# An attention block written out in ticks: each engine's result is taken up one tick later, and the first FFN quarter takes both chunks of a batch through each weight tile

## The chip, the cores and the metric

The kernel runs on one core of one Trainium2 chip. Its engines are TensorE (PE, matrix products), VectorE (DVE), ScalarE (ACT), GpSimd (POOL) and SyncE (SP, which here only issues transfers). Each engine works through its own list of instructions in the order in which the program was written, and waits at the head of that list for semaphores of the others. The metric is the device time of one execution in microseconds (us), lower is better.

## The reference

Three layers follow each other, all in float32. Batch 2, 8 heads, 768 positions, head size 64, so 512 channels.

```python
# attention: a window of +-15 positions, and 24 summary keys (max over 32 keys) with their mean values
scores_l = scale * q @ k.T                      # kept where |i - j| < 16
scores_s = scale * q @ k_sum.T + log(32)
a = softmax(concat(scores_l masked, scores_s))  # with 1e-9 added to the sum
x = a @ concat(v, v_sum)
# mixing over positions of rank 32, then a feed-forward network (FFN) 512 -> 2048 -> 512
u = x + (x.T @ U @ V).T
x = u + relu(u @ w_ch1) @ w_ch2
# second block: each position mixed with the one before it
xk = mu_k * x + (1 - mu_k) * x_prev;  xr = mu_r * x + (1 - mu_r) * x_prev
out = sigmoid(xr @ w_r) * (relu(xk @ w_k) ** 2 @ w_v)
```

## The kernel before

**Stages.** Attention runs per pair of heads: four pairs make a batch, and a pair is cut into three groups of 256 queries, so `attention(b)` has twelve groups. `attention(0)` runs alone. Then the first of four FFN quarters (512 hidden channels, four tiles of 128) is done for batch 0, and `attention(1)` is laid between its matrix products. After that come the same quarter for batch 1, three more quarters for both batches, and the second block. Weights come as 64-bit words and are converted on the way: loaded (L404), split by ACT (L415, L416), worked on by DVE (L421, L424, L425), added by POOL (L431), rounded to a high part by ACT (`whi`, L456) and a low part by POOL (`wlo`, L460). Each product of the FFN is three matmuls (high x high, high x low, low x high).

**One group of attention.** `s_stage` (L179): PE forms the scores of a group in two PSUM banks. `soft_stage` (L201): DVE adds the mask and takes the maximum (L208), ACT the exponential (L212), four times each. `t_stage` (L215): PE transposes, ACT copies to `pt` (L221). `v_stage` (L224): PE multiplies with the window's values `vcat` (L234), and DVE divides by the sum (L238, L239). Once per pair: `k_prep` (L136), in which DVE takes the summary keys `ks` (L140) and POOL lays windows and summary keys out in `kw` (L146 to L148); `sum_v` (L152, `vs`) and `spread_v` (L158), in which DVE sums values, PE turns them, ACT scales them into `vm` (L163) and POOL copies them to `vcat` (L164); and the mixing over positions, `g_stage`, `g2_stage`, `u_stage` (L251 to L287), whose results are `uhi` and `ulo`. In the first pair `turn_v` makes the window values on PE and ACT; other pairs load them (`load_vw`).

**What sets the order.** A plan of ticks, one per group (L301 to L381). In tick i stand the scores and soft stage of group i, the transpose of group i-2, the product with the values of group i-4 and parts of the mixing; then the steps that are not PE's (loads, `k_prep`, `sum_v`) and `d`, which takes so many slots from `side`, the list of weight conversions. A slot moves each of its blocks one step through load, ACT, DVE, POOL, ACT and POOL. The numbers in `at(tick, when, ...)` sort the steps of a tick. After `attention(0)` the FFN's generators give the order: after each half of an FFN tile (`f1`, into the hidden layer, or `f2`, out of it), two steps of `attention(1)` follow, and 1.2 slots of `side`.

**PSUM.** Eight banks, four under each of two names. `gen` holds scores and the products of `f1`, `acc` the accumulators of `f2` and, in `attention(0)`, transposes, values and mixing. In `attention(1)` all attention steps use `gen`. A step that needs a bank waits until the last reader of what stood there is through. For `f1` the last reader is DVE's subtraction to `hl` (L494).

Of the kernel before, what the change touches and what calls it, by code (L numbers as in the profile page):

```python
# [23 lines left out]
R = 32  # L24
# [38 lines left out]
def build(tc, I, out):  # L63
# [34 lines left out]
    vcat = [a_p.tile([128, NT, 2, D + 1], F32, name=f"vcat{i}", bufs=1) for i in range(3)]  # L98

    T_AT, V_AT = 2, 4  # L100
    NPT = V_AT - T_AT + 1
    pts = [a_p.tile([128, 512], F32, name=f"pt{i}", bufs=1) for i in range(NPT)]
# [7 lines left out]
    for i in range(3):  # L110

        nc_p.memset(vcat[i][KW:KC + 1], 0.0)
        nc_p.memset(vcat[i][:, :, :, D:D + 1], 1.0)
# [19 lines left out]
    def load_vw(n):  # L133
        nc.sync.dma_start(out=vcat[n % 3][0:KW], in_=I["vw"][n])
# [23 lines left out]
    def spread_v(n, tag):  # L158

        ps = bank(tag)  # L160
        nc_t.matmul(ps[KW:KC, 0:128], vs_t.pop(n), ident, start=True, stop=True)
        vm = a_p.tile([128, 2, D], F32, name="vm", bufs=2)
        nc_s.activation(vm[KW:KC].rearrange("p h d -> p (h d)"), ps[KW:KC, 0:2 * D], AF.Copy, scale=1.0 / BLK)  # L163
        nc_p.tensor_copy(vcat[n % 3][KW:KC, :, :, 0:D], vm[KW:KC].unsqueeze(1).to_broadcast([NB, NT, 2, D]))  # L164

    def turn_v(n, g, tag):

        ps = bank(tag)
        for j in range(4):
# [3 lines left out]
            vcat[n % 3][0:KW, 4 * g:4 * g + 4, :, 0:D], ps[0:KW].rearrange("p (t h d) -> p t h d", t=4, h=2)  # L173
# [3 lines left out]
    pt_t = {}  # L177

    def s_stage(n, g, tag):  # L179

        ps = [bank(tag) for _ in range(2)]
# [17 lines left out]
        return ps  # L199

    def soft_stage(n, g, ps):  # L201
        P = a_p.tile([128, 4, KC], F32, name="P", bufs=T_AT + 1)
        nm = a_p.tile([128, 4], F32, name="nm", bufs=3)
        for j in range(4):
# [6 lines left out]
            )  # L211
            nc_s.activation(P[:, j], P[:, j], AF.Exp, bias=nm[:, j:j + 1], scale=-1.0)  # L212
        p_t[n, g] = P

    def t_stage(n, g, tag):  # L215
        P = p_t.pop((n, g))
# [3 lines left out]
        pt = pts[(3 * n + g) % NPT]  # L220
        nc_s.copy(pt[0:KC], ps[0:KC])  # L221
        pt_t[n, g] = pt

    def v_stage(n, g, tag):  # L224
        if g == 0:
            x_t[n] = x_p.tile([128, NP, 128], F32, name="xn", tag="xn", bufs=2)
# [3 lines left out]
        for a in range(2):  # L230
            for h in range(2):
                for e in range(2):
                    o = (2 * a + h) * 128 + 64 * e
                    nc_t.matmul(  # L234
                        o4[64 * e:64 * e + 64, a, h], pt[0:KC + 1, o:o + 64], vcat[n % 3][0:KC + 1, 4 * g + 2 * a + e, h], start=True, stop=True,
                    )
        rec = a_p.tile([128, 2, 2, 1], F32, name="rec", bufs=3)
# [22 lines left out]
    def g2_stage(n, tag):  # L260
# [5 lines left out]
        nc_v.tensor_tensor(  # L266
            out=gst[2 * R:3 * R], in0=ps[2 * R:3 * R, 0:128], in1=gst[2 * R:3 * R].bitcast(F32), op=ALU.subtract
# [3 lines left out]
    def u_stage(n, c, tag):  # L271
# [15 lines left out]
        nc_v.tensor_tensor(out=ulo[:, d], in0=ps[:, 0:CH], in1=uhi[:, d].bitcast(F32), op=ALU.subtract)  # L287
# [13 lines left out]
    def attention(b):  # L301

        pairs = range(4 * b, 4 * b + 4)
# [6 lines left out]
        end = len(groups)  # L310
        for i, (n, g) in enumerate(groups):
            at(i, 0, "s", n, g)
            if b or i < end - 4:
                at(i + T_AT, 1, "t", n, g)
                at(i + V_AT, 4, "v", n, g)
                if g == NG - 1:
                    for j, t in enumerate(G_AT):
                        at(i + V_AT + t[0], t[1], "u", n, j)
        if b == 0:

            n = pairs[-1]
            for tick, when, what, *args in (
                (end - 2, 1, "t", n - 1, 2), (end - 1, 1, "t", n, 0), (end, 0.0, "v", n - 1, 2), (end, 1.0, "t", n, 1),
                (end, 1.2, "t", n, 2), (end, 2.0, "v", n, 0), (end, 2.2, "u", n - 1, 0), (end, 2.4, "v", n, 1),
                (end, 2.6, "u", n - 1, 1), (end, 2.8, "v", n, 2), (end, 3.0, "u", n - 1, 2), (end, 3.2, "u", n, 0),
                (end, 3.3, "u", n - 1, 3), (end, 3.4, "u", n, 1), (end, 3.5, "u", n, 2), (end, 3.6, "u", n, 3),
            ):
                at(tick, when, what, *args)
        for n in pairs:
            i = 3 * (n - 4 * b)  # L330
            at(i + 1, 4.5, "sp", n)
            for g in range(NG if n < N_TR else 0):
                at(i + 1 + g, 4.6, "tv", n, g)
        steps = [
# [5 lines left out]
        ]  # L340
        if b:
            steps = []
            for n in range(pairs[1], pairs[-1] + 1):
                steps += [
                    (3 * n - 15, (("k", n), ("lk", n + 1), ("lq", n + 1))), (3 * n - 14, (("sv", n), ("lt", n + 1))),
                    (3 * n - 12, (("lv", n + 1),)),
                ]
        for t, jobs in steps:
            for j, (what, n) in enumerate(jobs):
                if what == "d" or n < 4 * B:  # L350
                    at(t, 6 + 0.1 * j, what, n)
        for tick in sorted(plan):
            steps = sorted(plan[tick], key=lambda x: x[0])
            soft = None
            for k, (_, what, args) in enumerate(steps):
                n = args[0]
                if what in side_steps:
                    side_steps[what](*args)
                    continue
                if what == "s":  # L360
                    soft = (*args, s_stage(*args, tags["s"]))
                    if k + 1 < len(steps) and steps[k + 1][1] == "t":
                        continue
# [469 lines left out]
```

## Time and profile before

| | |
|---|---|
| median of three runs | 557.81 us (556.53 to 558.03) |
| the profiled execution | 555.79 us, span of its instructions 554.0 us |
| PE busy | 519.1 us, 94% of the span |
| DVE, ACT, POOL busy | 316.7, 251.6 and 210.6 us |
| `attention(0)`, until the first FFN matmul | 0 to 60.5 us |
| first FFN quarter of batch 0 with `attention(1)` | 60.5 to 138.6 us |
| all the rest | 138.6 to 554.0 us |

The profiled execution took 1.8 us more than its span; its time is 2.0 us under the median of the three runs. A busy engine is not yet an engine at its peak: PE has two clock levels (1.2 and 2.4 GHz), and at the lower one the same matmul takes about twice as long and still counts as busy. The row of granted clocks tells the level.

### The profile page before, as it was taken

The page shows a single profiled execution, that of the slowest core. Times are in us where ns is not written, and L with a number is a line of the kernel's source. Part 1 is how long each engine was busy: PE and PEld are TensorE (multiplying, and loading weights), DVE is VectorE, ACT ScalarE, POOL GpSimd, SP SyncE. Part 2 cuts the span into 40 slices and gives each one's busy share as a digit, 9 for nine tenths or more (in the row PEclk, how much of TensorE's full clock was granted, in tenths as well). Part 3 has the DMA queues.
Part 4 walks back from the last instruction along what each step waited for, and adds up shares of the span by engine and source line. Part 5 has one row for each costly group of instructions (what it writes and reads, how often), then busy time and mean ns, then how long its engine had stood idle before and what let it go on. Part 6 is the DMA issues. An engine that isn't in the chain of part 4 may idle for free.

```text
span 554.0 us, 8939 instructions
## 1 busy us (share of the span) xinstructions
PE 519.1 (94%) x3468; PEld 475.6 (86%) x3468; DVE 316.7 (57%) x703; ACT 251.6 (45%) x532; POOL 210.6 (38%) x190
## 2 busy tenths in 40 slices
PE   5777488999999999999999999999999999999997
PEld 4555365887999999999999999999888888888885
DVE  5686767544376267755778247746676542542322
ACT  4768366542245144543554144533558543542221
POOL 6354365330077936662666236214352120120000
PEclk9979869999999999999999999999999999999999
DMA  8962393200043023341343123012200100100101
GB/s 270 315 207 77 93 309 108 76 2 1 1 146 127 32 76 117 112 144 48 114 153 112 41 76 115 1 37 78 77 0 1 57 2 0 58 0 1 57 1 57
DMA packets 15129, 45.71 MB, mean 83 GB/s; under 512 B 2656, under 2 KB 2912, under 8 KB 15088
## 3 DMA queue, kind: packets, MB, share of 16 engines
q1 hardware_dynamic: 14912, 44.92, 24.9%
q8 instruction: 27, 0.44, 0.3%
q10 hardware_dynamic: 144, 0.18, 0.2%
q14 instruction: 14, 0.11, 0.1%
q0 software_dynamic: 32, 0.05, 0.0%
HBM read 42.00 MB, written 3.15 MB: 81 GB/s over the span
## 4 chain that ended last, share of the span: by engine, by line
PE 83%; DVE 6%; ACT 5%; DMA 2%; POOL 2%; issue 1%; SPq 0%; POOLq 0%; ACTq 0%; DVEq 0%
PE acc L510 24%; PE gen L489 24%; PE gen L607 12%; PE acc L629 12%; PE gen L591 5%; ACT P L212 2%; DMA kt<-kt 2%; PE gen L196 1%; PE gen L234 1%; PE gen L219 1%; POOL vcat L164 1%; DVE C L424 1%; DVE P L208 1%; PE acc L234 1%; DVE A L425 1%
## 5 line engine op out<-in xcount | busy, mean ns | idle before, releaser
L431 POOL TENSOR_TENSOR A<-C,A 128x512 int32<-128x512 int32 (+1 forms) x54 | 70.9, 1313 | 99.3 <-DVE A L425 97.7
L460 POOL TENSOR_TENSOR wlo<-A,whi 128x512 fp32r<-128x512 f32 x52 | 75.7, 1456 | 49.3 <-ACT whi L456 49.1
L489 PE MATMUL gen<-uhi,whi 128*128 128x384 f32 x256 | 88.3, 345 | 0.0
L510 PE MATMUL acc<-hh,whi 128*128 128x384 f32 x256 | 87.5, 342 | 0.6 <-ACT hh L493 0.6
L489 PE MATMUL gen<-uhi,wlo 128*128 128x384 f32 x256 | 87.0, 340 | 0.0
L489 PE MATMUL gen<-ulo,whi 128*128 128x384 f32 x256 | 86.9, 340 | 0.0
L510 PE MATMUL acc<-hh,wlo 128*128 128x384 f32 x256 | 86.6, 338 | 0.0
L510 PE MATMUL acc<-hl,whi 128*128 128x384 f32 x256 | 86.6, 338 | 0.0
L494 DVE SCALAR_TENSOR_TENSOR hl<-gen,hh 128x384 fp32r<-128x384 f32 x64 | 35.6, 556 | 88.3 <-ACT hh L493 88.3
L493 ACT ACTIVATE hh<-gen 128x384 fp32r<-128x384 f32 x64 | 31.3, 489 | 103.6 <-PE gen L489 103.5
L611 DVE TENSOR_TENSOR kt<-kt 128x384 f32<-128x384 f32 x32 | 20.4, 636 | 64.9 <-ACT kt L610 64.9
L425 DVE SCALAR_TENSOR_TENSOR A<-stg,A 128x512 int32<-128x512 int32 (+1 forms) x54 | 52.1, 965 | 0.0
L489 PEld LDWEIGHTS gen<-uhi,whi 128*128 128x128 f32 x256 | 48.7, 190 | 1.2 <-issue 1.0
L510 PEld LDWEIGHTS acc<-hh,whi 128*128 128x128 f32 x256 | 48.1, 188 | 1.7 <-ACT hh L493 0.9
L489 PEld LDWEIGHTS gen<-ulo,whi 128*128 128x128 f32 x256 | 48.7, 190 | 0.0
L489 PEld LDWEIGHTS gen<-uhi,wlo 128*128 128x128 f32 x256 | 48.7, 190 | 0.0
L510 PEld LDWEIGHTS acc<-hl,whi 128*128 128x128 f32 x256 | 48.1, 188 | 0.0
L510 PEld LDWEIGHTS acc<-hh,wlo 128*128 128x128 f32 x256 | 48.1, 188 | 0.0
L456 ACT CAST whi<-A 128x512 fp32r<-128x512 f32 x52 | 32.3, 620 | 32.0 <-POOL A L431 31.5
L607 PE MATMUL gen<-xkl,whi 128*128 128x384 f32 x128 | 43.3, 338 | 0.6 <-POOL xkl L569 0.6
L607 PE MATMUL gen<-xkh,whi 128*128 128x384 f32 x128 | 43.2, 338 | 0.0
L607 PE MATMUL gen<-xkh,wlo 128*128 128x384 f32 x128 | 43.2, 337 | 0.0
(127 smaller groups left out, 983.5 us busy)
## 6 DMA issues: line engine op xcount, KB each, us to landing
stg<-w SPq DMA_DIRECT2D x32, 512.0 KB, 3.3
stg<-wk SPq DMA_DIRECT2D x8, 512.0 KB, 3.2
stg<-wv SPq DMA_DIRECT2D x8, 512.0 KB, 3.3
vcat<-vw SPq DMA_DIRECT2D x7, 585.0 KB, 8.1
kt<-kt SPq DMA_DIRECT2D x8, 384.0 KB, 7.9
vt<-vt SPq DMA_DIRECT2D x8, 384.0 KB, 8.6
out<-sig SPq DMA_DIRECT2D x12, 256.0 KB, 2.1
qt<-qt SPq DMA_DIRECT2D x7, 384.0 KB, 10.8
```

What stands on the lines that cost most here:

```text
L425: nc_v.scalar_tensor_tensor(out=a, in0=st[i]["raw"][:, :, 1], scalar=-2 ** 31, in1=a, op0=ALU.bitwise_and, op1=ALU.bitwise_or)
L431: nc_p.tensor_tensor(out=a, in0=c, in1=a, op=ALU.add)
L456: nc_s.copy(wt[key][0], w)
L460: nc_p.tensor_tensor(out=lo, in0=w, in1=hi.bitcast(F32), op=ALU.subtract)
L489: nc_t.matmul(ps, w[:, sl], x[:, k], start=(n == 0), stop=(n == 3 * KD - 1))
L493: nc_s.activation(hh, ps, AF.Relu)
L494: nc_v.scalar_tensor_tensor(out=hl, in0=ps, scalar=0.0, in1=hh.bitcast(F32), op0=ALU.max, op1=ALU.subtract)
L510: nc_t.matmul(acc[d], w[:, sl], x, start=(i == 0 and n == 0), stop=(i == FT - 1 and n == 2))
L591: nc_t.matmul(ps, x[:, k, sl], w, start=(n == 0), stop=(n == 3 * KD - 1))
L607: nc_t.matmul(ps, w[:, sl], x[:, k], start=(n == 0), stop=(n == 3 * KD - 1))
L611: nc_v.tensor_tensor(out=t, in0=t, in1=t, op=ALU.mult)
L629: nc_t.matmul(acc, x[:, sl], w, start=(f == 0 and n == 0), stop=(f == KFT - 1 and n == 2))
```

## The change

**Attention.** The soft stage is cut in two: `score_stage` (DVE's part) stands in the tick of the scores, or one tick later in batch 0, whose scores now run one tick ahead; `exp_stage` (ACT's part) stands a tick after that. Transposes stand in tick i+2, values in tick i+3 (i+4 before). What DVE does with a PSUM result of the same step (dividing, `gst`, `ulo`) is no longer written behind that step: it goes to a list `late` and is written at the start of the next tick (batch 0, `fl`) or ahead of the next PE step (batch 1). The mixing steps of a pair stand in four ticks that follow each other. `k_prep` of pairs 2 and 3 comes ahead of `spread_v` of the pair before them, and the loads of pairs 4 and 5 and `k_prep(4)`, `sum_v(4)` ahead of the last three conversion slots. There are two `vcat` buffers (three before) and two `pt` (three before); `vcat` loads stand later, and the low part of `V` is made by POOL, not DVE.

**FFN.** `hl` is written ahead of the next `f1` or `f2`, not behind its own `f1`. For batch 0's first quarter `first_units` takes both chunks c of 384 positions through tile i of `w1` before it goes on, so that the first four `f1` need two weight tiles. The conversion order follows that. Attention steps begin after the fourth half tile, one slot of `side` per half tile.

```diff
-    T_AT, V_AT = 2, 4
+    vcat = [a_p.tile([128, NT, 2, D + 1], F32, name=f"vcat{i}", bufs=1) for i in range(2)]
+    late = deque()
+    def flush():
+        while late:
+            late.popleft()()
...
-            nc_s.activation(P[:, j], P[:, j], AF.Exp, bias=nm[:, j:j + 1], scale=-1.0)
+    def exp_stage(n, g):
+        P, nm = p_t[n, g]
+        for j in range(4):
+            nc_s.activation(P[:, j], P[:, j], AF.Exp, bias=nm[:, j:j + 1], scale=-1.0)
...
+        late.append(lambda: norm_stage(n, g, o4))
...
-                at(i + T_AT, 1, "t", n, g)
-                at(i + V_AT, 4, "v", n, g)
+            at(i - ahead, 1, "s", n, g)
+            at(i, 2, "score", n, g)
+            for lag, when, what, left in ((1, 3, "exp", 1), (2, 4, "t", 2), (3, 5, "v", 3)):
...
-            (12, (("d", 3), ("lv", 4), ("lk", 5), ("lq", 5), ("lt", 5), ("lv", 5), ("k", 4), ("sv", 4))),
+                (12, (("lv", 5), ("k", 4), ("sv", 4), ("d", 3))),
...
-        nc_v.tensor_tensor(out=vst[r, c], in0=w[r], in1=vst[r, c].bitcast(F32), op=ALU.subtract)
+        nc_p.tensor_tensor(out=vst[r, c], in0=w[r], in1=vst[r, c].bitcast(F32), op=ALU.subtract)
...
+    def first_units():
+        for i in range(FT):
+            for c in range(NC):
+                yield from f1(0, 0, c, i, keep=c > 0 and i < FT - 1)
+                yield
+            if i:
+                yield from f2(0, 0, 0, i - 1)
+                yield
+        for c, i in [(0, FT - 1)] + [(1, i) for i in range(FT)]:
+            yield from f2(0, 0, c, i)
+            yield
...
-    run(both(chain(ffn_unit(0, 0, 0), ffn_unit(0, 0, 1)), tail, 2), 1.2)
+    run(both(first_units(), tail, 2, 3), 1.0)
```

Three places show what this makes of the order. On PE at the start of the program, before (L196 scores, with `kt` and `ks` in the first pair; L161 `spread_v`; L171 `turn_v`; L219 transposes):

```order
L196 MATMUL gen<-kt_112,qt 64x96 x8
L196 MATMUL gen<-ks,qt 64x24 x8
L161 MATMUL acc<-ident,vs 24x128
L171 MATMUL acc<-ident,vt_115 96x128 x4
L196 MATMUL gen<-kt_112,qt 64x96 x8
L196 MATMUL gen<-ks,qt 64x24 x8
L219 MATMUL acc<-ident,P 120x128 x4
L171 MATMUL acc<-ident,vt_115 96x128 x4
L196 MATMUL gen<-kw_111,qt 64x120 x8
```

and in the change, from the second group's scores on (L200 scores, L168 `turn_v`, L158 `spread_v`, L227 transposes):

```order
L200 MATMUL gen<-kt_110,qt 64x96 x8
L200 MATMUL gen<-ks,qt 64x24 x8
L168 MATMUL acc<-ident,vt_113 96x128 x4
L158 MATMUL acc<-ident,vs 24x128
L200 MATMUL gen<-kw_109,qt 64x120 x8
L227 MATMUL acc<-ident,P 120x128 x4
```

The first `spread_v` moved behind the third group's scores and the first `turn_v`, and the first transposes and the second `turn_v` moved behind the scores of pair 1. On POOL in `attention(0)`, before (pairs 0, 1 and 2; `vcat<-vm` waits for `spread_v`):

```order
L164 COPY vcat_104<-vm 24x24x64
L146 COPY kw_111<-kt_113 128x12x32
L147 COPY kw_111<-kt_113 128x12x64
L148 COPY kw_111<-ks 128x12x24
L164 COPY vcat_105<-vm 24x24x64
L146 COPY kw_110<-kt_114 128x12x32
L147 COPY kw_110<-kt_114 128x12x64
L148 COPY kw_110<-ks 128x12x24
```

and in the change:

```order
L161 COPY vcat_104<-vm 24x24x64
L143 COPY kw_109<-kt_111 128x12x32
L144 COPY kw_109<-kt_111 128x12x64
L145 COPY kw_109<-ks 128x12x24
L143 COPY kw_108<-kt_112 128x12x32
L144 COPY kw_108<-kt_112 128x12x64
L145 COPY kw_108<-ks 128x12x24
L161 COPY vcat_105<-vm 24x24x64
```

Pair 2's `kw` moved ahead of pair 1's `vcat<-vm`; pair 1's stayed behind pair 0's. On DVE where the FFN begins, before (the last `ulo`, two conversions, then `ks` and `vs` of pair 4 and the first scores of `attention(1)`; tile numbers are kept here to tell the conversions apart):

```order
L287 TENSOR_TENSOR ulo_621<-acc_890,uhi_620 128x384
L421 TENSOR_SCALAR C_770<-C_770 128x512
L424 TENSOR_SCALAR C_770<-C_770 128x512
L425 SCALAR_TENSOR_TENSOR A_769<-stg_529,A_769 128x512
L421 TENSOR_SCALAR C_908<-C_908 128x512
L424 TENSOR_SCALAR C_908<-C_908 128x512
L425 SCALAR_TENSOR_TENSOR A_907<-stg_648,A_907 128x512
L140 TENSOR_REDUCE ks_923<-kt1_113 128x24
L156 TENSOR_REDUCE vs_928<-vt0_115 128x24
L208 ISA P_949,nm_950<-gen_939,mask_95 128x120
```

and in the change, right behind the last `ulo` (the next row is the first L212 of `attention(1)`, the scores' mask and maximum):

```order
L137 TENSOR_REDUCE ks_898<-kt1_111 128x24
L153 TENSOR_REDUCE vs_903<-vt0_113 128x24
L428 TENSOR_SCALAR C_806<-C_806 128x512
L431 TENSOR_SCALAR C_806<-C_806 128x512
L432 SCALAR_TENSOR_TENSOR A_805<-stg_545,A_805 128x512
L428 TENSOR_SCALAR C_916<-C_916 128x512
L431 TENSOR_SCALAR C_916<-C_916 128x512
L432 SCALAR_TENSOR_TENSOR A_915<-stg_669,A_915 128x512
L428 TENSOR_SCALAR C_939<-C_939 128x512
L431 TENSOR_SCALAR C_939<-C_939 128x512
L432 SCALAR_TENSOR_TENSOR A_938<-stg_801,A_938 128x512
L511 SCALAR_TENSOR_TENSOR hl_949<-gen_927,hh_948 128x384
```

The summary keys moved ahead of the conversions, the conversions before the first scores of `attention(1)` became three, and the `hl` of the first `f1` now stands behind all of them and directly ahead of those scores. On PE the second group of scores of `attention(1)` takes a bank that this `hl` frees.

## Rows read from the trace of the kernel before

**Rows 1.** Windows by stage: length, busy us (instructions) by engine, clock, DMA share.

```profile
0.00:60.50 60.50, 42.82 (x589) 32.30 (x590) 39.82 (x160) 38.51 (x100) 27.06 (x41) 0.92 0.62 199
60.50:81.50 21.00, 12.90 (x109) 9.60 (x107) 16.34 (x49) 10.44 (x27) 12.22 (x14) 0.67 0.81 246
81.50:138.60 57.10, 53.06 (x580) 44.13 (x578) 31.37 (x120) 28.65 (x77) 19.04 (x19) 1.00 0.18 52
138.60:554.00 415.40, 410.34 (x2196) 389.59 (x2195) 229.14 (x376) 174.03 (x330) 152.24 (x116) 1.00 0.18 61
```

**Rows 2.** Windows inside attention(0) and the first FFN tiles, same columns.

```profile
25.30:49.50 24.20, 19.30 (x258) 13.91 (x259) 20.21 (x78) 16.85 (x45) 10.90 (x11) 0.79 0.48 164
...
25.40:31.60 6.20, 6.16 (x69) 4.33 (x69) 5.33 (x18) 4.55 (x11) 2.35 (x2) 0.50 0.66 225
...
49.50:60.50 11.00, 8.97 (x125) 7.09 (x124) 6.08 (x19) 6.75 (x18) 3.07 (x3) 1.00 0.16 49
...
68.10:81.50 13.40, 11.69 (x102) 8.71 (x102) 8.99 (x40) 7.55 (x21) 7.07 (x9) 0.56 1.02 311
```

**Rows 3.** Waits, first 140 us: engine, line, releaser, total us, times, longest.

```profile
PE gen L196 <- POOL kw L148: 10.6, 3, 6.4
...
PE acc L285 <- DVE gst L266: 4.6, 3, 2.6
```

**Rows 4.** Timeline of PE: start, duration, instruction, [idle before <-releaser].

```profile
14.02 1.17 PE L196 MATMUL gen<-kw,qt 64*64 64x120 f32 x16 [0.28 <-POOL kw L148]
...
19.67 0.64 PE L196 MATMUL gen<-kw,qt 64*64 64x120 f32 x16
...
25.44 1.08 PE L196 MATMUL gen<-kw,qt 64*64 64x120 f32 x16 [3.93 <-POOL kw L148]
...
60.48 0.34 PE L489 MATMUL gen<-uhi,whi 128*128 128x384 f32 x1
...
68.14 1.46 PE L196 MATMUL gen<-kw,qt 64*64 64x120 f32 x18 [6.43 <-POOL kw L148]
```

**Rows 5.** Timeline of POOL: vcat and kw of attention(0), then first FFN wlo.

```profile
21.67 2.02 POOL L164 COPY vcat<-vm 24x1536 f32<-24x1536 f32 x1 [7.71 <-ACT vm L163]
...
24.96 0.42 POOL L148 COPY kw<-ks 128x288 f32<-128x288 f32 x1
...
61.75 1.46 POOL L460 TENSOR_TENSOR wlo<-A,whi 128x512 fp32r<-128x512 f32 x1 [9.10 <-ACT whi L456]
```

**Rows 6.** Lines of DVE in attention(0): shapes xcount, busy us, mean ns.

```profile
L208 DVE CUSTOM_DVE_ANT_0 P<-gen,mask 128x120 f32<-128x120 f32 x48 | 10.6, 276 | 5.1 <-PE gen L196 5.0
...
L239 DVE TENSOR_TENSOR xn<-acc,rec 128x256 f32<-128x256 f32 x12 | 5.1, 424 | 0.4
...
L425 DVE SCALAR_TENSOR_TENSOR A<-stg,A 128x512 int32<-128x512 int32 (+1 forms) x5 | 3.4, 670 | 0.0
...
L421 DVE TENSOR_SCALAR C<-C 128x512 f32<-128x512 f32 (+1 forms) x5 | 2.7, 550 | 0.7 <-ACT C L416 0.7
...
L674 DVE TENSOR_TENSOR vst<-A,vst 32x320 fp32r<-32x320 f32 (+1 forms) x2 | 2.3, 1149 | 0.1
...
L424 DVE TENSOR_SCALAR C<-C 128x512 int32<-128x512 int32 (+1 forms) x5 | 2.1, 420 | 0.2
```

**Rows 7.** Timeline of DVE behind the last ulo.

```profile
61.66 0.42 DVE L421 TENSOR_SCALAR C<-C 128x512 f32<-128x512 f32 x1
...
62.11 1.38 DVE L424 TENSOR_SCALAR C<-C 128x512 int32<-128x512 int32 x1
...
64.01 0.41 DVE L421 TENSOR_SCALAR C<-C 128x512 f32<-128x512 f32 x1
...
66.66 0.94 DVE L140 TENSOR_REDUCE ks<-kt 128x24 f32<-128x768 f32 x1
```

**Rows 8.** Chain of waits: an f1 behind the attention.

```profile
142.76 2.09 PE gen L489 x12
```

**Rows 9.** Page's transfers: queue, count, KB each, us to landing.

```profile
vcat<-vw SPq DMA_DIRECT2D x7, 585.0 KB, 8.1
```

More of the change, by code (lines that the diff above doesn't have):

```diff
@@ L109, in build @@
         eng.memset(t[:, WIN + S:], 0.0)
-    for i in range(3):
-        nc_p.memset(vcat[i][KW:KC + 1], 0.0)
-        nc_p.memset(vcat[i][:, :, :, D:D + 1], 1.0)
+    for vc in vcat:
+        nc_p.memset(vc[KW:KC + 1], 0.0)
+        nc_p.memset(vc[:, :, :, D:D + 1], 1.0)
     kw_t = {}
@@ L133, in load_vw @@
     def load_vw(n):
[L134 removed]
+        nc.sync.dma_start(out=vcat[n % 2][0:KW], in_=I["vw"][n])
     def k_prep(n):
@@ L177, in build @@
     pt_t = {}
+    s_t = {}
+    late = deque()
+    def flush():
+        while late:
+            late.popleft()()
     def s_stage(n, g, tag):
-        ps = [bank(tag) for _ in range(2)]
+        ps = s_t[n, g] = [bank(tag) for _ in range(2)]
         q = q_t[n]
@@ L286, in u_stage @@
         nc_s.copy(uhi[:, d], ps[:, 0:CH])
-        nc_v.tensor_tensor(out=ulo[:, d], in0=ps[:, 0:CH], in1=uhi[:, d].bitcast(F32), op=ALU.subtract)
+        late.append(
+            lambda: nc_v.tensor_tensor(out=ulo[:, d], in0=ps[:, 0:CH], in1=uhi[:, d].bitcast(F32), op=ALU.subtract)
+        )
     def y_stage(b):
@@ L310, in attention @@
         end = len(groups)
+        ahead = int(b == 0)
         for i, (n, g) in enumerate(groups):
-            at(i, 0, "s", n, g)
-            if b or i < end - 4:
-                at(i + T_AT, 1, "t", n, g)
-                at(i + V_AT, 4, "v", n, g)
-                if g == NG - 1:
-                    for j, t in enumerate(G_AT):
-                        at(i + V_AT + t[0], t[1], "u", n, j)
+            at(i - ahead, 1, "s", n, g)
+            at(i, 2, "score", n, g)
+            for lag, when, what, left in ((1, 3, "exp", 1), (2, 4, "t", 2), (3, 5, "v", 3)):
+                if b or i < end - left:
+                    at(i + lag, when, what, n, g)
@@ L319, in attention @@
+        for n in pairs:
+            i = 3 * (n - pairs[0])
+            at(i + 1, 6.2, "sp", n)
+            for g in range(NG if n < N_TR else 0):
+                at(i + 1 + g, 6.1, "tv", n, g)
+            for j, what in enumerate(("g", "g2", "u", "u")):
+                if b or n < pairs[-2]:
+                    at(i + 6 + j, 6, what, n, *([j - 2] if what == "u" else []))
         if b == 0:
+            for t in range(end + 1):
+                at(t, 0, "fl")
             n = pairs[-1]
[L322 to L326, printed above, removed]
-            ):
-                at(tick, when, what, *args)
@@ new lines, in attention @@
+            steps = (
[6 rows of a table added]
+            )
+        else:
+            steps = []
+            for n in pairs[1:]:
+                i = 3 * (n - pairs[0])
+                steps += [(i - 2, (("k", n),)), (i, (("sv", n),))]
+                if n < pairs[-1]:
+                    steps += [(i - 2, (("lk", n + 1), ("lq", n + 1), ("lt", n + 1))), (i + 2, (("lv", n + 1),))]
+        for t, jobs in steps:
+            for j, job in enumerate(jobs):
+                at(t, 7 + 0.1 * j, *job)
+        on_pe = {
+            "s": (s_stage, "s"), "t": (t_stage, "t"), "v": (v_stage, "v"), "sp": (spread_v, "v"), "tv": (turn_v, "v"),
+            "g": (g_stage, "v"), "g2": (g2_stage, "v"), "u": (u_stage, "v"),
+        }
```

153 lines of the change are left out of this document (69 added, 84 removed), and 9 rows, old and new, of the table steps.

## Prediction, made before the changed kernel was run

> **What bounds the kernel now.** I read the windows by stage first [rows 1]. From 138.6 us on PE is busy 410.34 of 415.40 us at the full clock: nothing is to be had there, and the change leaves that stretch its amount of work. What can move lies in the first 138.6 us, in three pieces. In `attention(0)`, 0 to 60.5 us, PE is busy 42.82. In the first 21 us of the FFN it is busy 12.90, most of it at the lower clock: 11.69 at a mean granted clock of 0.56 [rows 2] is 6.5 us of full-clock work, with the other 1.21 at the full clock it makes 7.7, so that 13.3 of 21 us are lost. From 81.5 to 138.6 only 57.10 - 53.06 = 4.0 are lost.
>
> Second, the waits [rows 3]: PE waited three times for POOL's `kw`, 10.6 us in all, and three times for `gst` before the product with it, 4.6. The timeline of PE says where [rows 4]: 3.93 us before the scores of pair 2 (25.44), and 6.43 before the first scores of `attention(1)` (68.14). Behind each the clock is low: 0.50 from 25.4 to 31.6, though PE was busy 6.16 of 6.20 us [rows 2]. One scores group takes 1.08 us at that level (25.44) and 0.64 at the upper one (19.67) [rows 4].
>
> Third, DVE: from 25.3 to 49.5 it is busy 20.21 of 24.20 [rows 2]. With PE's waits gone, it is the next to bind.
>
> **Part A: `attention(0)` in ticks.** In the first ticks the order loses a little. `spread_v` now stands behind one scores group and one `turn_v` more, POOL's `vcat<-vm` waits for it, and pair 1's `kw` stands behind that copy. Before, PE waited 0.28 us for this `kw` at 14.02 [rows 4]; the cost lies between nothing and two PE steps, some 2 us by the 1.17 of that row. I take 0.5. One `turn_v`, about 1 us at the lower clock, comes behind it. Against that stands the wait for pair 2's `kw`. POOL had stood in front of `vcat<-vm` for 7.71 us, copied until about 23.7, and finished `kw` at 24.96 + 0.42 = 25.4 [rows 5]. In the change this `kw` is ahead of the copy, so PE's scores of pair 2 are due when PE gets there: 25.44 - 3.93 = 21.5 as it was, + 0.5, + 1.0 for the turn, + 0.6 for more steps at the lower clock = 23.6. That is 1.8 us earlier than before.
>
> From there DVE sets the pace, as I see it. It had 20.21 us of work in 24.20. Work comes forward into this stretch, since the values now stand three ticks behind, not four: two normalisations at 0.42 [rows 6] and a reciprocal of some 0.2 each, one group of scores at about 0.8 (four of 276 ns, overlapping), one `gst` of 0.3, and one conversion of 0.55 + 0.42 + 0.67 = 1.6, taken as 1.5 [rows 6]: 3.8. The subtraction for `V` (L674), 2.3 us, goes to POOL [rows 6]. So 21.7 us of DVE work follow 23.6. With none of the old 4.0 us of idle time the last scores end at 45.3, with all of it at 49.3; I take the middle, 47.3 (49.5 before).
>
> The tail behind the last scores took 11.0 us, in which PE was busy 8.97 [rows 2]; the rest was mainly waiting for `gst`, which with `late` and a tick between is covered. In the change one product with `gst` less (0.7, with its `xn` transposes) and one group of transposes more (0.5) belong to it, and about 1.2 of it, a group of transposes and one of values, is done while the last scores are still on DVE: 7.6 and a small wait, 7.7. The FFN then starts at 47.3 + 7.7 = 55.0, a gain of 5.5. The bounds are 45.3 + 6.3 (one more group through by then) = 51.6 and 49.3 + 11.0 = 60.3, which is gains of 8.9 and 0.2.
>
> **Part B: the first FFN half tiles.** Let T0 be the first FFN matmul. Before, six matmuls ran, and then PE stood until 68.14 because DVE did two conversions between the last `ulo` and pair 4's `ks`: 64.01 - 61.66 = 2.35 and 66.66 - 64.01 = 2.65 [rows 7]. In the change `ks` and `vs` come at once, and PE has two whole `f1` (2.09 each [rows 8]) and one scores group to do, 4.8 us. Then comes the new wait. The second scores of `attention(1)` need the bank that the first `hl` frees, and DVE does that `hl` behind three conversions. `ulo` ends 1.2 after T0 (61.66 against 60.48 [rows 4, 7]), `ks` and `vs` take 1.75 (0.94 for the first [rows 7], the second overlapping a little), the conversions 3 x 2.5, `hl` half a microsecond: T0 + 11.0. Queued behind `hl` on DVE stand the first scores' masks, for which ACT's exponentials wait and later the transposes. With conversions of 1.64, as in `attention(0)` [rows 6], it is T0 + 8.4; that is the lower bound of the wait, and the upper one is 14, if each takes 3.5.
>
> From T0 + 11 PE goes on at the lower clock, as it did from 68.1 to 81.5 [rows 2]: nine microseconds to T0 + 20 give 4.5 of work, 9.3 with the first 4.8. Lost are 10.7 against 13.3, a gain of 2.6 to 2.7 (from +7 where the wait ends early and the clock stays up, to -1 where it ends at T0 + 14).
>
> Why a conversion takes 1.6 here and 2.5 there is told by one pair of rows: L424 takes 1.38 us at 62.11 while POOL makes `wlo` from 61.75 to 63.21, and 0.42 in the mean [rows 5 to 7]. The Trainium skill ("SBUF — State Buffer", section "Who interferes with whom") says that DVE and GpSimd share a pair of memory ports as an exclusive lock, so that the one who comes second is blocked for the whole instruction; the trace agrees for this pair, 1.38 against 0.42. By that rule the three conversions in a row cost what POOL has to do beside them, and POOL has `kw` and three `wlo` and `A` to do there: the sum would be the one with 2.5 or more. If POOL came off lightly it would be the one with 1.64, T0 + 8.4, and some 1.5 us less in all.
>
> **Part C: the rest of the first quarter.** There 4.0 us are lost [rows 1]. The steps are spread one slot per half tile, and results taken a step later; I take 3.0, a gain of 1.0, between a loss of 2 and a gain of 3. In the remaining 415 us `hl` stands behind the next half tile's start: its reader is then a whole `f1` or `f2` away, 2.09 us or more [rows 8], and I cost it at nothing. Were that cover gone, each of some 60 `hl` would cost part of its half microsecond, up to 10 us in all; but between an `f1` and its reader stands a whole `f2`. Two `vcat` buffers instead of three make a load wait for the last values of the pair before the last. It lands in 8.1 us [rows 9] and has about four ticks, 13 us: nothing, or up to 3 us on the one that is late.
>
> **The sum.** 5.5 + 2.7 + 1.0 = 9.2. The profiled execution took 555.8, so 546.6; the median of the three runs stands 2.0 above that execution, so 548.5.
>
> **The rivals.** First, more gain: DVE loses all its idle time, the FFN starts at 51.5 (-9.0), the conversions are quick and the clock stays up, 7.5 lost in part B (-5.8), and C gives 1.0: -15.8, or 542.0. For it speaks that most of DVE's waits in `attention(0)` are for PE's scores (5.0 us [rows 6]); against it, that so many small waits go at once. Second, the bank wait eats part B: `hl` comes at T0 + 14, 16.3 are lost (+3.0), C gains nothing, A stays: 555.3 or so. For it speaks the 2.65 conversion with the rows of POOL beside it; against it, that only one of three has to wait for weights. Third, the ticks do not do what they say: PE, DVE and ACT end each tick waiting on one another as before, `attention(0)` ends at 59.5, and only B and C give something: 1.0 + 2.7 + 1.0 = 4.7, or 553.0. Fourth, slower: PE is left at the lower clock. If each tick ends in a short wait for DVE, PE's steps take 1.08 for 0.64, a tick of five steps some 5.2 us where DVE needs 3.3, so +1.9 per tick, and PE becomes the bound. In the trace the clock was low for the two ticks behind the 3.93 wait and then rose while PE stayed busy [rows 2, 4]. Over the ten ticks left this is +19 in `attention(0)`, less the 9.2 of the forecast: 567.6. It decides from about five such ticks on, when the low level lasts past 40 us. The Trainium skill ("TensorE: Matmul & The Clock Gate", section "HAM oscillation — how this bites in real kernels") describes such a loop, bursts of matmuls with waits between them that fall back to half the clock each time; here one long wait was followed by it, and no row shows ticks with short waits doing so.
>
> **How the numbers follow.** Forecast 0.50 (its own range 544 to 552.5, from half of each term's bounds), more gain 0.20, bank wait 0.12, ticks without effect 0.09, low clock 0.09. The range is 540 to 557: it takes in the first three rivals and leaves out the low clock and a little at both ends. A difference of 0.3%, 1.7 us, is about what a measurement of this kernel can tell from none. Faster by more: nearly all of the forecast, all of the first, half of the second and nearly all of the third, 0.84. Within: 0.07. Slower: 0.09.
>
> **What would show it.** The first FFN matmul at about 55 us (A); no wait over 1 us for `kw` at pair 2; DVE busy over nine tenths between 24 and 47; PE idle from about T0 + 4.8 to T0 + 11, ended by the first `hl` or by scores of DVE (B); `hl` waits of the later FFN without PE idle behind them (C). It is wrong if the FFN starts past 59, if the granted clock is low over most of `attention(0)`, or if PE's idle time past 138.6 grows by more than 2 us.

## The result, and the profile after

The changed kernel takes 549.61 us (median of four runs, 548.71 to 551.85), the kernel before, beside it, 557.17; the ratio is 0.987 (95% interval 0.9835 to 0.9905). A second measurement of the same two kernels gave 0.9883 (0.9838 to 0.9928). The forecast was 548.5. The profiled execution took 548.71, its span is 546.9 us against 554.0.

Windows of the changed kernel, as in [rows 1]: `attention(0)` up to the first FFN matmul, then up to the point from which PE has the same 410.34 us of work left as the kernel before had at 138.60, then the rest; the last row is a stretch inside `attention(0)`.

```profile
0.00:55.74 55.74, 39.48 (x588) 29.20 (x589) 39.24 (x157) 38.11 (x100) 28.07 (x43) 1.00 0.79 259
55.74:129.32 73.58, 63.93 (x674) 52.47 (x674) 45.95 (x164) 37.27 (x98) 30.20 (x31) 0.95 0.25 79
129.32:546.90 417.58, 410.35 (x2209) 388.93 (x2207) 229.20 (x379) 175.62 (x335) 152.37 (x116) 1.00 0.18 61
21.80:46.20 24.40, 18.95 (x286) 13.21 (x284) 23.61 (x91) 22.48 (x62) 14.98 (x14) 1.00 0.80 263
```

So 60.5 + 78.1 + 415.4 became 55.7 + 73.6 + 417.6: -4.7, -4.5 and +2.2. PE's timeline answers [rows 4]:

```profile
14.04 1.18 PE L200 MATMUL gen<-kw,qt 64*64 64x120 f32 x16 [3.72 <-POOL kw L145]
...
17.03 1.08 PE L200 MATMUL gen<-kw,qt 64*64 64x120 f32 x16
...
19.81 0.64 PE L200 MATMUL gen<-kw,qt 64*64 64x120 f32 x16
...
21.91 0.64 PE L200 MATMUL gen<-kw,qt 64*64 64x120 f32 x16
...
55.74 0.34 PE L503 MATMUL gen<-uhi,whi 128*128 128x384 f32 x1
...
60.03 0.64 PE L200 MATMUL gen<-kw,qt 64*64 64x120 f32 x16
67.23 1.76 PE L200 MATMUL gen<-kw,qt 64*64 64x120 f32 x16 [6.56 <-DVE hl L511]
```

The reader is to see three things. The wait for pair 2's `kw` (25.44 in [rows 4]) is gone, its scores start at 21.91. In its place stands one for pair 1's `kw`, 3.72 us at 14.04. And the FFN runs two whole `f1` and one scores group, then stands for 6.56 us until the first `hl` frees the bank. DVE around that `hl`, as in [rows 7]; the last row is the `hl` of the second `f1`:

```profile
58.64 1.25 DVE L428 TENSOR_SCALAR C<-C 128x512 f32<-128x512 f32 x1
...
60.87 0.42 DVE L428 TENSOR_SCALAR C<-C 128x512 f32<-128x512 f32 x1
61.32 1.37 DVE L431 TENSOR_SCALAR C<-C 128x512 int32<-128x512 int32 x1
62.61 0.68 DVE L432 SCALAR_TENSOR_TENSOR A<-stg,A 128x512 int32<-128x512 int32 x1
64.28 0.43 DVE L428 TENSOR_SCALAR C<-C 128x512 f32<-128x512 f32 x1 [0.99 <-ACT C L423]
...
66.63 0.54 DVE L511 SCALAR_TENSOR_TENSOR hl<-gen,hh 128x384 fp32r<-128x384 f32 x1
67.10 0.27 DVE L212 CUSTOM_DVE_ANT_0 P<-gen,mask 128x120 f32<-128x120 f32 x1
...
70.33 0.55 DVE L511 SCALAR_TENSOR_TENSOR hl<-gen,hh 128x384 fp32r<-128x384 f32 x1
```

From 58.64 to 66.63 DVE does three conversions, 8.0 us with a wait of 0.99 for ACT. DVE is not all that holds this `hl`: the `hh` that it reads comes late too, since on ACT it stands behind a weight rounding that waits for POOL:

```profile
62.44 0.62 ACT L463 CAST whi<-A 128x512 fp32r<-128x512 f32 x1 [4.37 <-POOL A L438]
...
64.08 0.48 ACT L509 ACTIVATE hh<-gen 128x384 fp32r<-128x384 f32 x1
```

So with no conversion ahead of it on DVE alone, this `hl` could not have begun before about 64.6, some 2 us earlier than it did.

What the rest lost is one row of the waits from 131 us on; the kernel before had no wait for `y` on PE there:

```profile
PE acc L529 <- DVE y L537: 2.3, 2, 1.5
```

### The profile page after: what moved, and what is told of

Its sections match the earlier page's. It is cut to its first block, busy times and chain, and to the rows that moved or that the text cites. A ratio compares the mean times of both kernels' runs of the same rounds, so it can differ in the third digit from the quotient of the medians.

```text
span 546.9 us, 8932 instructions
## 1 busy us (share of the span) xinstructions
PE 513.8 (94%) x3468; PEld 470.6 (86%) x3468; DVE 314.4 (57%) x700; ACT 251.0 (46%) x532; POOL 210.6 (39%) x190
## 4 chain that ended last, share of the span: by engine, by line
PE 80%; DVE 7%; POOL 5%; ACT 5%; issue 1%; DMA 1%; SPq 0%; POOLq 0%; DVEq 0%; ACTq 0%
PE acc L529 23%; PE gen L503 21%; PE gen L639 12%; PE acc L661 12%; PE gen L623 5%; PE gen L200 2%; POOL A L438 2%; POOL wlo L467 1%; DVE C L428 1%; PE gen L240 1%; DVE A L432 1%; DVE C L431 1%; ACT P L221 1%; POOL vcat L161 1%; PE gen L227 1%
## 5 line engine op out<-in xcount | busy, mean ns | idle before, releaser
L511 DVE SCALAR_TENSOR_TENSOR hl<-gen,hh 128x384 fp32r<-128x384 f32 x64 | 35.5, 555 | 65.7 <-ACT hh L509 65.7
L432 DVE SCALAR_TENSOR_TENSOR A<-stg,A 128x512 int32<-128x512 int32 (+1 forms) x54 | 54.1, 1002 | 0.0
L428 DVE TENSOR_SCALAR C<-C 128x512 f32<-128x512 f32 (+1 forms) x54 | 32.0, 592 | 23.3 <-ACT C L423 21.9
```

Source lines behind the costliest of these rows:

```text
L428: nc_v.tensor_scalar(out=c_f, in0=c_f, scalar1=as_float(0x38000000), scalar2=as_float(0x47EFFE00), op0=ALU.max, op1=ALU.min)
L432: nc_v.scalar_tensor_tensor(out=a, in0=st[i]["raw"][:, :, 1], scalar=-2 ** 31, in1=a, op0=ALU.bitwise_and, op1=ALU.bitwise_or)
L511: lambda: nc_v.scalar_tensor_tensor(out=hl, in0=ps, scalar=0.0, in1=hh.bitcast(F32), op0=ALU.max, op1=ALU.subtract)
```

## The experiments

All are edits of the changed kernel. Ratios are to the kernel before on the same chip; the stages are those of one profiled execution each, cut as above (the first quarter ends where PE has 410.34 us of work left), in us.

| | ratio (95% interval) | FFN start | first quarter | rest |
|---|---|---|---|---|
| the change | 0.987 (0.9835 to 0.9905) | 55.7 | 73.6 | 417.6 |
| change_again | 0.9883 (0.9838 to 0.9928) | 55.7 | 75.0 | 418.4 |
| attn_only | 0.9994 (0.9979 to 1.0008) | 55.5 | 78.9 | 416.9 |
| hl_now | 1.0005 (0.9976 to 1.0034) | 56.7 | 77.7 | 418.8 |
| hl_first | 0.9829 (0.9793 to 0.9866) | 55.7 | 71.4 | 417.6 |
| k1_first | 0.9803 (0.9785 to 0.982) | 50.7 | 74.9 | 418.0 |
| filler | 0.984 (0.9784 to 0.9896) | 54.0 | 73.5 | 417.6 |
| vst_dve | 0.9897 (0.9869 to 0.9924) | 56.2 | 73.7 | 417.8 |
| no_clamp | 0.9848 (0.9803 to 0.9892) | 56.6 | 72.6 | 418.0 |
| exp_half | 0.9907 (0.9868 to 0.9945) | 55.8 | 73.6 | 417.6 |
| rate07 | 0.9848 (0.9816 to 0.988) | 56.1 | 73.5 | 416.1 |
| combo | 0.9683 (0.9647 to 0.9719) | 51.0 | 69.6 | 416.7 |
| combo_k | 0.9711 (0.9643 to 0.9779) | 51.4 | 70.4 | 416.2 |

The cut goes by PE's busy time, and in change_again and k1_first it misleads: behind a wait for `y` the clock fell there, the work behind the cut took longer, and the cut moved to a later point. In change_again:

```profile
176.97 0.41 PE L529 MATMUL acc<-hh,whi 128*128 128x384 f32 x1 [2.31 <-DVE y L537]
...
178.20 0.52 PE L529 MATMUL acc<-hh,whi 128*128 128x384 f32 x1
```

The last product with `gst` of `attention(1)` starts 78.8 us behind the first FFN matmul in the change, 78.7 in change_again and 78.6 in k1_first. So the first quarter is the same in all three, and what change_again and k1_first have more, 2.3 and 1.9 us, lies in the rest. Two executions of one kernel differ that much in the rest; a difference of this size there in one trace is not read as an effect without a row that shows it.

The FFN start needs a second look too. From the third scores group of pair 1 (19.81 in the change) to the first FFN matmul 35.9 us pass in the change, and 35.9 to 36.0 in change_again, attn_only, hl_now, hl_first, filler and rate07; what differs between their FFN starts came about before that group.

**change_again.**

> The changed kernel itself, so that the others are compared with it on one chip. Every theory: a ratio to the kernel before of 0.984 to 0.990.

As expected: 0.9883. Its trace adds one thing: the clock fell here also in the middle of `attention(0)`, behind a wait of 1.57 us at 32.74, where the change's own trace has 0.69 and 0.64 for the same blocks:

```profile
34.73 1.14 PE L240 MATMUL acc<-vcat,pt 121*64 121x65 f32 x16
...
36.95 1.08 PE L200 MATMUL gen<-kw,qt 64*64 64x120 f32 x16
```

It cost nothing: the FFN starts at 55.7 in both.

**attn_only: the attention part alone.**

```diff
-    first_blocks += [blocks[i] for i in (0, 2, 1, 4, 3, 6, 5, 7)]
+    first_blocks += blocks
-    run(both(first_units(), tail, 2, 3), 1.0)
+    run(both(chain(ffn_unit(0, 0, 0), ffn_unit(0, 0, 1)), tail, 2, 0), 1.2)
-        hid_late.append(lambda: nc_v.scalar_tensor_tensor(out=hl, ...))
+        nc_v.scalar_tensor_tensor(out=hl, ...)
```

> The attention part of the change alone: the FFN's first quarter, its weight order, its 1.2 slots and hl right behind its f1 are as before. Theory (two separate gains: the ticks bring the first FFN matmul forward by 4.7 us, the two chunks per weight tile give the rest): FFN start at 55.7 as in the changed kernel, and the time about 2 to 4 us longer than the changed kernel, 551.5 to 553.5. Rival (the new FFN order gives nothing, because the wait before the second scores took over what it saved): no difference from the changed kernel, 549 to 550.5.

Neither: the FFN starts at 55.5, 5 us before the kernel before, and the time is the same as before, 0.9994. The first quarter takes 78.9 us, and PE waits in it, as it did in the kernel before, mostly for masks and `kw` (1.3 us more are for `hl`):

```profile
PE gen L200 <- DVE nm L212: 6.2, 2, 4.8
PE gen L200 <- POOL kw L145: 4.4, 2, 2.9
```

In this trace the earlier start is 5.0 us, 0.8 of it is lost in the first quarter and 1.5 in the rest; the profiled execution (553.05) was the fastest of ten, and of the median's missing gain the trace shows no more than that. So the attention part shows no gain without the other one. The reverse, the FFN part without the attention part, was not run, so how much of the gain the FFN part would bring alone stays open.

**hl_now: only the late writing of `hl` undone.**

```diff
-        hid_late.append(lambda: nc_v.scalar_tensor_tensor(out=hl, ...))
+        nc_v.scalar_tensor_tensor(out=hl, ...)
```

> The changed kernel with hl written right behind its own f1, as before. Theory (writing it later costs nothing past the first quarter, and in the first tiles the wait for its bank shrinks by one conversion of the three): the stretch behind the attention stays at 417.6 us within 0.7, the 6.56 us wait falls to 3.5 to 5, time 0 to 2.5 us less than the changed kernel. Rival (late hl is what brings the PE waits for the y sums): these waits, 2.3 us, go.

Both fell, and this is the largest surprise: the whole gain of the change is gone (1.0005). The first `hl` stands ahead of the first masks in both kernels; here DVE meets the second one, too, before these masks (in the change it stands behind them, at 70.33). At each of the two it waits for ACT's `hh`, which is itself behind the weight rounding that waits for POOL. DVE, and then PE, in this kernel:

```profile
63.57 0.67 DVE L432 SCALAR_TENSOR_TENSOR A<-stg,A 128x512 int32<-128x512 int32 x1
65.51 0.56 DVE L510 SCALAR_TENSOR_TENSOR hl<-gen,hh 128x384 fp32r<-128x384 f32 x1 [1.26 <-ACT hh L509]
...
68.79 0.56 DVE L510 SCALAR_TENSOR_TENSOR hl<-gen,hh 128x384 fp32r<-128x384 f32 x1 [0.84 <-ACT hh L509]
69.26 0.27 DVE L212 CUSTOM_DVE_ANT_0 P<-gen,mask 128x120 f32<-128x120 f32 x1
```

```profile
66.12 0.66 PE L200 MATMUL gen<-kw,qt 64*64 64x120 f32 x2 [4.56 <-DVE hl L510]
69.40 1.07 PE L200 MATMUL gen<-kw,qt 64*64 64x120 f32 x14 [2.62 <-DVE hl L510]
...
84.22 0.65 PE L227 MATMUL gen<-ident,P 128*120 128x128 f32 x4 [0.60 <-DVE hl L510]
...
94.84 0.69 PE L240 MATMUL gen<-vcat,pt 121*64 121x65 f32 x16 [0.74 <-DVE hl L510]
```

One wait of 6.56 became two of 7.2 together: the second scores stop after two matmuls until the second `hl` is done. Smaller waits for `hl` follow in the whole quarter, 2.7 us more. The first quarter takes 77.7 us; with 0.9 at the start and 1.2 in the rest (less than two executions of the change differ by there) the trace is 6.3 us longer than that of the change. The waits for `y` stay (2.7 us), so late `hl` is not what brings them. The later FFN start (56.7) is not the edit's: the scores of pair 1 came 0.4 us later, and the low clock behind them lasted longer, which cost another 0.5. The old order of the `f1` with late `hl` was not run, so these runs show that the gain needs the late `hl`, not that it needs the new order.

**hl_first: no conversions ahead of the first `hl`.**

```diff
-                (12, (("lv", 5), ("k", 4), ("sv", 4), ("d", 3))),
+                (12, (("lv", 5), ("k", 4), ("sv", 4))),
-    run(both(first_units(), tail, 2, 3), 1.0)
+    run(both(first_units(), tail, 2, 3), 1.0, -3.0)
-    def run(gen, rate):
-        due = 0.0
+    def run(gen, rate, due=0.0):
```

> The changed kernel without the three conversion slots at the end of attention(0) and without slots in the first three FFN half tiles, so that on DVE hl of the first f1 and the first masks come right behind ks and vs of pair 4, ahead of all conversions. Theory (PE's wait of 6.56 us before the second scores is the conversions ahead of hl on DVE): the wait falls under 1.5 us, the FFN start stays at 55.7, the time falls by 3 to 5 us, to 545 to 547. Rival (the engines must do the conversions and the first scores in these 20 us anyway, and the next step waits for them instead): another wait of the same size appears within 10 us, the time stays within 1 us of the changed kernel.

The wait is gone, as the theory had it: 0.71 us is left, for a mask. But more than half of it comes back. PE's rows, and windows of this kernel (56 to 64, then 84 to 92):

```profile
61.48 0.64 PE L200 MATMUL gen<-kw,qt 64*64 64x120 f32 x14 [0.71 <-DVE nm L212]
...
84.38 1.08 PE L200 MATMUL gen<-kw,qt 64*64 64x120 f32 x16 [2.91 <-POOL kw L145]
```

```profile
56.00:60.00 4.00, 4.00 (x28) 3.75 (x27) 3.14 (x5) 0.86 (x2) 0.48 (x2) 1.00 0.42 133
60.00:64.00 4.00, 3.07 (x41) 2.11 (x40) 3.33 (x19) 2.26 (x7) 0.00 (x0) 1.00 0.29 92
...
84.00:92.00 8.00, 7.62 (x70) 6.31 (x74) 4.62 (x15) 2.77 (x8) 4.39 (x5) 0.60 0.07 18
```

At 84.38 PE waits 2.91 us for a `kw` that POOL makes behind the conversions it now does later, and the granted clock is 0.60 in the 8 us behind. Of 5.8 us taken from the wait, 2.1 remain. Theory and rival each have a part. The edit takes the slots away whole, from ACT and POOL as well as from DVE, so it does not tell DVE's conversions from ACT's late `hh`.

**k1_first: pair 1's `ks` and `kw` ahead of pair 0's `spread_v`.**

```diff
-                (0, (("sv", 0),)), (1, (("k", 1),)), (2, (("d", 3),)),
+                (0, (("sv", 0),)), (2, (("d", 3),)),
+            at(1, 0.5, "k", 1)
```

> The changed kernel with pair 1's ks and kw written ahead of pair 0's spread_v, so that POOL makes this kw before it waits for vcat<-vm. Theory (PE's 3.72 us before the scores of pair 1, ended at 14.04 by kw, is POOL standing behind vcat<-vm, and DVE, idle then, sets the pace later): the scores of pair 1 come 1 to 1.5 us earlier, and so does the FFN start, 548 to 548.6. Rival (what is won at 14 us is lost by 25 us, since later pairs' loads or DVE's work do not come earlier): the FFN start moves by less than 0.4 us.

More than the theory asked: the FFN starts 5.0 us earlier. PE, in this kernel:

```profile
10.35 0.91 PE L200 MATMUL gen<-kw,qt 64*64 64x120 f32 x16 [0.92 <-DVE nm L212]
...
12.22 0.64 PE L200 MATMUL gen<-kw,qt 64*64 64x120 f32 x16
```

The scores of pair 1 come 3.7 us earlier, and the blocks behind take 0.64 at once, where the change has 1.08 until 18 us. That raised a question, which the next run answers.

**filler: the wait left, but PE busy in it.**

```diff
+        if n == 0:
+            fill = bank(tag)
+            for j in range(16):
+                nc_t.transpose(fill[0:KW, j % 4 * 128:(j % 4 + 1) * 128], vt_b[0][:, j % 4 * TQ:j % 4 * TQ + KW], ident)
```

> The changed kernel with 16 extra transposes on PE (results unused) in the 3.72 us in which it waits for pair 1's kw, so that PE is busy there and the wait itself stays. Theory (of the 5.0 us that k1_first brought the FFN start forward, 3.7 are the wait and the rest the clock, which stood at the lower level until 18 us behind this wait): the scores of pair 1 still come at 14.0 to 14.3, its blocks take 0.64 to 0.9 instead of 1.08, and the FFN starts 1 to 1.5 us earlier than 55.7. Rival (the clock there costs nothing, since PE waits for DVE and ACT behind it anyway): FFN start within 0.4 us.

The theory holds. `kw` comes at 14.08 as ever, but PE, which waited 1.84 us instead of 3.72, goes on at the upper level:

```profile
10.29 1.95 PE L162 MATMUL acc<-ident,vt 128*96 128x128 f32 x16
14.08 0.74 PE L204 MATMUL gen<-kw,qt 64*64 64x120 f32 x16 [1.84 <-POOL kw L145]
...
15.77 0.64 PE L204 MATMUL gen<-kw,qt 64*64 64x120 f32 x16
```

The FFN starts at 54.0, 1.7 us earlier, for work that is thrown away; every later block is 1.7 us earlier, too (the third scores group of pair 1 at 18.11, not 19.81). The time alone would not show it, since the intervals of the ratio overlap. If the clock weighs as much in k1_first, 1.7 of its 5.0 us are the clock and about 3.3 the wait; no run separates the two there.

**vst_dve, no_clamp, exp_half: does DVE or ACT set the pace in `attention(0)`?**

```diff
-        nc_p.tensor_tensor(out=vst[r, c], ...)          # vst_dve
+        nc_v.tensor_tensor(out=vst[r, c], ...)
-            nc_v.tensor_scalar(out=c_f, ..., op0=ALU.max, op1=ALU.min)   # no_clamp: not in the first ten blocks
-        for j in range(4):                               # exp_half
+        for j in range(4 if n > 3 else 2):
```

> The changed kernel with the low part of V (two subtractions, 2.3 us in the trace of before) back on DVE. Theory (from 22 to 46 us DVE is the bound in the changed kernel): the last scores and the FFN start come 1.2 to 2.3 us later, 550.8 to 551.9. Rival (the chain PE, DVE, ACT, PE of a tick sets the pace, with DVE's idle time only hidden): under 0.5 us.

> The changed kernel without the clamp (L428) in the conversions of the first ten blocks, which limits the size of the weights' bits and is left out of the computation: DVE has 3.5 us less to do between 21 and 45 us, and 2.1 us less between the last ulo and the first hl. Theory (DVE sets the pace in both places): FFN start 2.5 to 3.5 us earlier, the 6.56 us wait before the second scores 1.5 to 2.1 shorter, time 4 to 5.5 us less. Rival (in attention(0) it is the chain from engine to engine that sets the pace): FFN start less than 1 us earlier, the wait before the second scores shorter all the same, time 1 to 2.5 us less.

> The changed kernel in which ACT does two of the four exponentials of each group of batch 0 (the other two blocks keep their masked scores; so much is left out of the computation): 0.6 us less ACT work in each of twelve ticks, 7 us in all. Theory, formed after no_clamp and vst_dve (ACT, busy 22.5 of 24.4 us between 21.8 and 46.2, belongs to the chain that sets the pace of a tick, and DVE's amount of work does not): FFN start 2 to 5 us earlier. Rival (the pace is set by neither, but by PE with its waits, or by DVE after all): FFN start less than 1 us earlier.

DVE got 2.3 us more, then 3.5 less, then ACT 7 less, and the FFN start was 56.2, 56.6 and 55.8, against 55.7. Counted from the third scores group of pair 1, the stretch to the FFN is 36.3, 36.3 and 35.5 us, against 35.9: 0.4 longer, 0.4 longer and 0.4 shorter. The theory that one engine's amount of work sets the pace fell for DVE and for ACT. In no_clamp the last masks do come 0.8 us sooner after that group, but the tail behind them grew from 9.4 to 10.7. The windows from 21.8 to 46.2 suggest why: in the change DVE is busy 23.61 and ACT 22.48 of 24.40; without the clamp

```profile
21.80:46.20 24.40, 20.02 (x294) 13.75 (x289) 22.00 (x89) 21.89 (x61) 14.42 (x13) 0.93 0.79 264
```

DVE has more idle time, ACT is as full as before, and the chain that ended last passes from the conversions on DVE to ACT's exponentials (19.3% of it between 14 and 56 us, 9.4% in the change). With half the exponentials it passes back to DVE and to PE; PE's granted clock fell to 0.66 from 32 to 42 us (1.00 in the change, and 0.83 in change_again, which lost nothing by it):

```profile
32.00:42.00 10.00, 9.15 (x110) 6.65 (x110) 9.70 (x40) 5.59 (x14) 6.45 (x5) 0.66 0.74 245
```

That DVE and ACT bind together here, so that what is taken from one is met by the other, is the reading that is left; a run with less work on both, which would show it, was not made. In the FFN no_clamp did what both its theories said, in part: the wait before the second scores is 5.8 us, 0.8 shorter.

**rate07: 0.7 conversion slots per half tile behind the first quarter.**

```diff
-    run(chain(ffn_unit(0, 1, 0), ffn_unit(0, 1, 1)), 0.6)
+    run(chain(ffn_unit(0, 1, 0), ffn_unit(0, 1, 1)), 0.7)
```

> The changed kernel with 0.7 instead of 0.6 conversion slots per half tile in the run behind the first quarter of batch 0. Theory (first_units leaves no f2 over, so that this run has two half tiles fewer and does 18 of 21 slots, and the three that are drained in one go at its end hold back hh and with it the y sums, for which PE waits 0.8 and 1.5 us at 157.8 and 176.3): the 1.5 us wait goes, the 0.8 may, and the time falls by 1 to 2.3 us. Rival (the waits come from hl being written one half tile later): both waits stay, no difference.

Both waits for `y` are gone and the rest takes 416.1 us instead of 417.6. What is left of such waits in the stretch:

```profile
PE acc L529 <- ACT hh L509: 0.7, 1, 0.7
```

The intervals of the ratio overlap with the change's, so the time alone doesn't show the 1.5 us; the rows do. attn_only, which keeps the old order and hands the run behind it an `f2`, has one wait for `y` of 0.3 us, and hl_now, with the new order, has them all. So they come with the new order and its slots, not with late `hl`.

**combo and combo_k: the three gains together, and `kw` one tick earlier.**

```diff
-                steps += [(i - 2, (("k", n),)), (i, (("sv", n),))]           # combo_k, on top of combo
+                steps += [(max(i - 3, 0), (("k", n),)), (i, (("sv", n),))]
```

> k1_first, hl_first and rate07 together. If the three act in different stages, their gains add up: 3.6 + 2.2 + 1 to 2 us less than the changed kernel, a ratio to the kernel before near 0.974. Rival (DVE, POOL and ACT are what bounds the first FFN tiles, so that hl_first gives nothing once the FFN starts earlier): 0.978 to 0.980.

> combo, with k_prep of pairs 5 to 7 one tick earlier in attention(1). Theory (what is left in the first FFN quarter are two waits for kw of 1.77 and 2.91 us, in which POOL stands behind conversions and vcat<-vm): both waits fall under 0.5 us, time 2 to 4.5 us under combo's, a ratio to the kernel before of 0.960 to 0.965. Rival (the wait moves on to the conversions' whi or wlo or to vcat): within 1 us of combo.

combo adds up and somewhat more: 539.02 us, 0.9683, a version that beats both kernels. All three stages show it (51.0, 69.6, 416.7). combo_k loses the two waits for `kw` and gets three others, for `hl` (2.8, 1.1 and 1.0 us); it is no faster. Its rival was right about the time, but not about the place, which it had at `whi`, `wlo` or `vcat`.

## Why the prediction was right, point by point

**Size and sign.** Forecast -9.2 us in the profiled execution, measured -7.1: right in sign and within the range, with one term missed and two that were right for a reason that did not hold. In the second trace, change_again, it was -5.0, because the waits for `y` and the clock behind them cost 2.3 us more.

**Part A** (-5.5, measured -4.7). The removed wait for pair 2's `kw` and the path of it through POOL were as described. The new wait for pair 1's was priced at 0.5 us plus a turn, from the 14.02 of [rows 4]; the scores came at the forecast time, 14.04, but PE stood 3.72 us for them, because the first transposes and the second `turn_v` no longer stood in front of them, and filler shows that this cost 1.7 us of clock besides. The middle came out earlier than forecast (pair 2 at 21.91, not 23.6; the last masks end at 46.3, not 47.3), the tail longer (9.4, not 7.7), so that the forecast's 55.0 owes something to luck. The reason given, that DVE sets the pace, failed: with 2.3 us more and 3.5 us less work on DVE the stretch changed by 0.4 us, both times upwards. DVE is full, 23.61 of 24.40, but so is ACT; what sets the length there is not shown.

**Part B** (-2.7) and **part C** (-1.0), together -3.7, measured -4.5. The new wait is there, in its place: the bank, the `hl`, the three conversions ahead of it. T0 + 11.0 was forecast, it ended at T0 + 11.5 (67.23 - 55.74), and hl_first shows that the conversion slots are the cause by taking them away. The prediction counted them on DVE alone; ACT's `hh`, at 64.08, would have held the `hl` until about 64.6 even with DVE free. Behind it the clock was low for less time than I took from [rows 2]: the blocks are at 0.34 from 73.0 on, where the kernel before had 0.52 until 78.3.

What the prediction did not see is what the gain hangs on. It priced the late writing of `hl` as a possible cost and gave the gain to the order of the `f1`. hl_now keeps that order and loses everything: the gain needs the place of `hl` on DVE, one half tile later, which puts the second `hl` behind the first masks. Whether it also needs the order is not shown.

**The step that failed** is "In the remaining 415 us ... I cost it at nothing": 2.2 us came there, and so the prediction's last sign of being wrong (PE's idle time past 138.6 growing by more than 2 us: from 5.1 to 7.2) just came true. The cause was not the `hl`, but the conversions: `first_units` leaves no `f2` to the run behind it, which so has two half tiles fewer, leaves more slots to its end, and PE waits for `y` at 157.8 and 176.3; with more slots per half tile (rate07) these waits are gone, and 1.5 of the 2.2 us with them.

**The rivals.** More gain (542.0) did not come: DVE's idle time went, but the FFN did not start at 51.5. The bank wait did not eat the gain. The low clock came for 4 us behind the 3.72 wait and 5.5 behind the 6.56. In this trace it did not come in the ticks between, whose waits are short (the longest 1.6 us at 32.7); in change_again it did, behind that same wait, and the FFN start did not move. So PE was not the bound there, as this rival needed. The Trainium skill ("TensorE: Matmul & The Clock Gate", section "HAM oscillation — how this bites in real kernels") describes a loop in which bursts of matmuls fall back to half the clock behind each wait; in the two traces of the change the clock rose again within 6 us behind every such wait, and no loop set in.

## What to carry to other kernels

Where several engines work in ticks and each is nine tenths busy, look for the first late tick, not for the busiest engine: a wait of 3.7 us at 14 us cost 5.0 at the FFN's start, and 3.5 us less work on the busiest engine gave none. In an in-order queue, what waits for another engine goes behind what others wait for; the subtractions to `hl`, written one half tile earlier, cost as much as all of the change won. When a stage's order is changed, count what it hands to the stage behind: two half tiles fewer left conversion slots over, and 2 us were lost behind the stage whose order had been changed. And when a trace is cut by the work that is left, compare a fixed instruction as well: a low clock behind the cut moves it.

## What the runs showed of the hardware

The granted clock's row can miss a low stretch, seen here by the blocks' durations. From 14 to 18 us the change and no_clamp have the same rhythm (blocks of 1.08 us), and their records read 1.00 and 0.50:

```profile
14.00:18.00 4.00, 3.96 (x40) 3.01 (x40) 1.71 (x10) 1.45 (x4) 1.20 (x2) 1.00 1.00 287
```

```profile
14.00:18.00 4.00, 4.00 (x41) 2.99 (x41) 1.93 (x10) 1.67 (x5) 1.09 (x3) 0.50 1.01 293
```

The duration of a known block (0.64 or 1.08) tells the level more surely. And useless matmuls in a wait can pay: 16 transposes, 1.95 us on PE, brought the FFN forward by 1.7. A low stretch costs time only where PE is waited for: the one behind 14 us cost these 1.7, the one from 34.7 to 38 us in change_again cost nothing.

Taking an instruction out of DVE's list gives back less than its own time where POOL works beside it: without the clamp (0.42 us at 60.87 in the change) the second of the three conversions took 2.1 us from its first start to its last end, instead of 2.4. In the change its middle instruction took 1.37 us beside POOL's addition; in no_clamp the middle one took 0.41, and the last one, 0.68 in the change, 1.75. The Trainium skill ("SBUF — State Buffer", section "Who interferes with whom") says that a DVE instruction with two inputs in SBUF contends with one of GpSimd that reads it; 1.75 beside POOL's addition (61.42 to 62.80) against 0.68 agrees.

```profile
61.27 0.41 DVE L432 TENSOR_SCALAR C<-C 128x512 int32<-128x512 int32 x1
61.60 1.75 DVE L433 SCALAR_TENSOR_TENSOR A<-stg,A 128x512 int32<-128x512 int32 x1
```

```profile
61.42 1.38 POOL L439 TENSOR_TENSOR A<-C,A 128x512 int32<-128x512 int32 x1 [0.96 <-DVE A L433]
```
